# Split values, block means and scale maxima through a buffer in HBM

## The chip, the core and the metric

The kernel runs on one core of a Trainium2 chip. The time is the device time of one execution in microseconds (us). The core has five engines with an instruction queue each: TensorE (PE, with weight loads PEld), VectorE (DVE), ScalarE (ACT), GpSimd (POOL) and SyncE (SP). In this kernel SP computes nothing; it issues every DMA, in one order fixed at build time. An instruction that waits for a semaphore holds up all that stand behind it on its engine. Sixteen DMA engines move the data.

## The reference

Four batches of local attention with block means, then a feed-forward layer with weights shared by all tokens. B=4, H=8, S=768, D=64; 3072 tokens of 512 values; `w_in` 512x2048, `w_out` 2048x512; all float32.

```python
block, window = 32, 16
k_sum = k.reshape(B, H, nb, block, D).max(axis=3)      # 24 blocks of 32 keys
v_sum = v.reshape(B, H, nb, block, D).mean(axis=3)
scores_l = scale * q @ k.T                              # kept where |i-j| < 16
scores_s = scale * q @ k_sum.T + log(block)
a = softmax(concat(scores_l masked, scores_s))
attn = a @ concat(v, v_sum)
h = x @ w_in
out = (h * sigmoid(h)) @ w_out                          # x = attn, heads side by side
```

## The kernel before

A query tile has 128 tokens; it is worked as two halves of 64 (z=0, 1). A half sees 96 neighbouring keys (64 and 15 on either side, and two that pad) and 24 block means: 120 columns. Tiles are numbered s=0 to 23, six per batch (t=0 to 5). Batch 0 is computed in float32; batches 1 to 3 have q, k, values, probabilities and means split into a high and a low float16 part, and three matmuls take the place of one. The split needs a scale, a power of two above the largest magnitude of the batch.

The feed-forward layer takes 12 chunks of 256 tokens. Chunk 0 is float32; from chunk 1 on, weights and activations are split in the same way (line 838 is the first product, 851 the second). Chunks 10 and 11 use a form with seven products in place of eight (lines 926, 968). ACT and DVE compute the activation in between: tanh (863), a product (864), the high part (866), the low part (867).

A planner (`Plan`) sets the order on every engine: each step has a cost for every engine that may run it, the keys that it reads and writes, and a priority from the numbers of `TUNE`; a list scheduler then places the steps, and the order that it finds is the program's order. Its cost for a DMA step is a number in the code, `{"dma": 2100}` for the loads of values below.

Places that the change touches:

- `job_v` (444) makes the block sums of values of a batch from four loads `vR`, their largest magnitude (`am_max`), the scale (`v_scale`), and the split means, which a DMA transpose brings to `vmp` (460).
- `job_vn` (539) loads 256 rows of values (`vP`), splits them and leaves them in SBUF, in `vn_t` (printed as tile `v` in the trace), a ring of two that shares its memory with `v0_t`. A row of split values is 2048 bytes.
- `job_vs` (549) fills `vv` (part of the tile `first`), the value operand of tile s, in two buffers. It issues eight DMAs: four copies SBUF to SBUF out of `vn_t` (15, 81, 79 and 17 rows, the first or last from a zero-padded input at the ends of a batch) and four of 24 rows of means.
- `all_max` (246) takes a maximum over the 128 partitions on POOL. It is called once for the weights, three times for q and k, four times for the values (402, 429, 793).
- `job_a` (line 691) transposes the split probabilities by DMA, four times per tile; `job_c` (724) multiplies them with `vv`.

All inputs of batches 1 to 3 pass through `raw`, a ring of three stages.

Of the kernel before, what the change touches and what calls it, by code (L numbers as in the profile page):

```python
# [10 lines left out]
F32 = mybir.dt.float32  # L11
F32R = mybir.dt.float32r
F16 = mybir.dt.float16
# [46 lines left out]
ALLMAX = 1100  # L60
# [7 lines left out]
class Plan:  # L68
# [58 lines left out]
    def sweep(self, prio, on, back):  # L127
# [18 lines left out]
        while ready:  # L146
# [13 lines left out]
            if e == "pe" and not back:  # L160
                early = early and cols < self.BUSY
# [12 lines left out]
            else:  # L174
                stop = t + cost * (1.0 if e in ("pe", "dma") else self.MARGIN)
# [58 lines left out]
def local_attn_ffn(ctx: ExitStack, tc: tile.TileContext, qkT, qP, qF, kF, v, vR, vP, w, out):  # L234
# [11 lines left out]
    def all_max(out, in_):  # L246
        nc.gpsimd.partition_all_reduce(out, in_, P, bass_isa.ReduceOp.max)

# [3 lines left out]
    const = ctx.enter_context(tc.tile_pool(name="const", bufs=1))  # L252
    psum = ctx.enter_context(tc.tile_pool(name="psum", bufs=1, space=bass.MemoryType.PSUM))
# [52 lines left out]
    vn_t = [t.bitcast(F16).rearrange("p (a i c) -> p a i c", a=2, i=2) for t in v0_t]  # L306
    vmf_t = const.tile([P, 4, P], F16, name="vmf")
# [30 lines left out]
    count = {}  # L338

# [52 lines left out]
    def job_scale(b, prio):  # L392
# [9 lines left out]
        plan.op({"pool": ALLMAX}, lambda e: all_max(qc[:, 0:2], qm_t[:, 7:9]), r=["qm_q", "qm_k"], w=["qc"], prio=prio)  # L402
# [20 lines left out]

    def am_max(n, prio):
        plan.op({"dve": 73}, lambda e: nc.vector.tensor_reduce(out=am_t[:, 7:8], in_=am_t[:, :n], axis=AX.X, op=ALU.max), r=[("am", j) for j in range(n)], w=["am4"], prio=prio)

    def v_scale(b, prio):
        vs = vsc_t[b % 2]
        plan.op({"pool": ALLMAX}, lambda e: all_max(sc2[:, 0:1], am_t[:, 7:8]), r=["am4"], w=["sc2"], prio=prio)
# [14 lines left out]
    def job_v(b, prio):  # L444
# [15 lines left out]
        plan.op({"dma": 1250}, lambda e: nc.sync.dma_start_transpose(out=vmp_t, in_=vmf_t.rearrange("p a b -> p (a b)")), r=["vmf"], w=["vmp"], prio=prio)  # L460
# [78 lines left out]
    def job_vn(b, n, prio):  # L539
# [7 lines left out]
        plan.op({"dve": 1196}, lambda e: nc.vector.scalar_tensor_tensor(out=vn[:, :, 1], in0=flat, scalar=vsc[:, 0:1], in1=vn[:, :, 0], op0=ALU.mult, op1=ALU.subtract), r=key + [("vsc", b % 2)], w=vn_key(g % 2), prio=prio)  # L547

    def job_vs(s, prio):
        prio += nudge("vs", s)  # L550
        b, t = divmod(s, NTILE)
        if b == 0:
            return
        if t == 0:
            job_vn(b, 0, prio)
            job_vn(b, 1, prio)
        if t == 3:
            job_vn(b, 2, prio)
        vv = vv_t[s % 2]
        key = ("vv", s % 2)  # L560

        def rows(z, at, tile, first, n):
            if not 0 <= tile < NTILE:
                return vv[at:at + n, z].rearrange("p i c -> p (i c)").bitcast(F32), v[0, t if z == 0 else NTILE - 1, at:at + n, z, :]
            g = (b - 1) * (NTILE // 2) + tile // 2
            return vv[at:at + n, z], vn_t[g % 2][first:first + n, tile % 2]

        part = P - HALF + HALO
# [7 lines left out]
        slots = {((b - 1) * (NTILE // 2) + x // 2) % 2 for x in (t - 1, t, t + 1) if 0 <= x < NTILE}  # L576
        plan.op({"dma": 2100}, load, r=["vmp", "first"] + [k for x in slots for k in vn_key(x)], w=[key], prio=prio)
# [45 lines left out]
    def job_a(m, prio):  # L623
# [55 lines left out]
        for j, n in enumerate(ns):  # L679
# [11 lines left out]
            plan.op({"dma": 1250}, lambda e, tt=tt, pt=pt: nc.sync.dma_start_transpose(out=tt, in_=pt.rearrange("p a b -> p (a b)")), r=pkeys + ["third"], w=[ttk], prio=prio)  # L691
# [99 lines left out]
    def w_scale(prio):  # L791
        plan.op({"dve": 80}, lambda e: nc.vector.tensor_reduce(out=wx_t, in_=wm_t, axis=AX.X, op=ALU.max), r=[("wm", f, kind) for f in range(NFT) for kind in range(2)], w=["wx"], prio=prio)
        plan.op({"pool": ALLMAX}, lambda e: all_max(wc[:, 0:2], wx_t), r=["wx"], w=["wc"], prio=prio)
# [19 lines left out]
    def job_f(n, c, fs):  # L813
# [12 lines left out]
        def fill():  # L826
            nc.tensor.matmul(out=h[:, :CH], lhsT=unit[:, :P], rhs=unit, start=True, stop=True)

# [26 lines left out]
        for at, f in enumerate(fs):  # L855
            need = [("wf", f, 0)] if c == 0 else [("wh", f, 0), ("wl", f, 0)]
            if n < HALVES:
                for half in range(2):
                    cs = slice(half * P, half * P + P)
                    plan.op({"pe": 900}, ffn1(at, f, cs), r=[("xh", z, half), ("xl", z, half)] + need, w=[("bank", k, half)], prio=i, cols=2048, fill=fill)  # L860
            else:
                plan.op({"pe": 1800 if c == 0 else 1312}, ffn1(at, f, slice(0, CH)), r=xs + need + turn, w=bk(k) if at == 0 else [("bank", k, 1)], prio=i + at, cols=4096 if c == 0 else 3072, fill=fill)
# [66 lines left out]
    def job_fast(n, c, fs):  # L929
# [7 lines left out]
        def fill():  # L937
            nc.tensor.matmul(out=h[:, :CH], lhsT=unit[:, :P], rhs=unit, start=True, stop=True)

        for at, y in enumerate(fs):  # L940
            plan.op({"pe": 1312}, ffn1_pairs(h, at, y, z), r=[(x, z, half) for x in ("xh", "xl") for half in range(2)] + [("wh", y, 0), ("wl", y, 0), ("turn", n - 3)], w=bk(k) if at == 0 else [("bank", k, 1)], prio=i + at, cols=3072, fill=fill)
# [71 lines left out]
    def job_tail(n, c, fs):  # L1013
# [9 lines left out]
        def fill():  # L1023
            nc.tensor.matmul(out=h[:, :CH], lhsT=unit[:, :P], rhs=unit, start=True, stop=True)

        for at, f in enumerate(fs):
            plan.op({"pe": 1312}, ffn1_pairs(h, at, f, z), r=[(x, z, half) for x in ("xh", "xl") for half in range(2)] + [("wh", f, 0), ("wl", f, 0), ("turn", n - 3)], w=bk(k) if at == 0 else [("bank", k, 1)], prio=i + at, cols=3072, fill=fill)
# [132 lines left out]
TUNE = dict(quad=308.75, vd=-86.5, ws=818.0, s0=-738.75, wp=1594.25, wm=33.0, km=-55.75, w_dma=-1.5, w_dec=878.75, a0=-71.0, a1=-119.25, d1=-66.5, span=51.75, post=1866.5, ffn2=5.0, jc0=92.5, jc1=-1748.25, jx0=2.25, jx1=143.0, vs=617.5, qk=305.75, k=-1369.75, v=-54.75, v0=83.75, out=-4.5, first=1452.5)  # L1160
# [61 lines left out]
```

## Time and profile before

| | |
|---|---|
| time, median of 3 runs | 672.36 us (671.85 to 673.94) |
| profiled execution | 674.95 us, span 673.2 us |
| PE busy | 598.7 us, 89% of the span |
| DVE busy | 458.7 us, 68% |
| ACT busy | 342.6 us, 51% |
| POOL busy | 92.9 us, 14% |
| mean granted TensorE clock | 0.953 |

The span is what the trace covers; 1.75 us of the execution lie around it. [...] In the rows below, a time ahead of a row is in us from the span's start, and names such as `L574` are lines of the kernel before.

### The profile page before, as it was taken

How to read it: one execution, taken by the hardware profiler on the slowest of the kernel's cores; microseconds unless marked ns; L12 is line 12 of the kernel's file. 1: busy time of each engine (PE TensorE's matmuls, PEld its weight loads, DVE VectorE, ACT ScalarE, POOL GpSimd, SP SyncE). 2: the span in 40 equal slices, each digit the busy share in tenths (PEclk: the TensorE clock that was granted, in tenths of full speed). 3: DMA queues.
4: the chain of work that ended last, by engine and by line, in shares of the span. 5: the costliest groups of instructions: out<-in, count | busy, mean ns of one | idle time of the engine just before them, and what ended most of it. 6: DMA issues, size and time to landing. Idle time of an engine off the chain costs nothing.

```text
span 673.2 us, 15159 instructions
## 1 busy us (share of the span) xinstructions
PE 598.7 (89%) x5944; PEld 413.3 (61%) x5944; DVE 458.7 (68%) x1243; ACT 342.6 (51%) x837; POOL 92.9 (14%) x183
## 2 busy tenths in 40 slices
PE   8899999799749858996998876999996798999997
PEld 5667666466526525663665543666663566688886
DVE  6799897898074636982773643879857696255655
ACT  4899885565054541651554532545643554234342
POOL 4112002201000000000000000005222420031130
PEclk9999999799969969998999797999997899999999
DMA  8997612237544539636433536474473379000000
GB/s 342 417 418 284 201 56 87 77 101 92 117 129 124 118 123 140 157 81 83 127 98 101 144 72 97 109 183 44 141 78 103 46 88 80 1 32 1 33 1 31
DMA packets 64938, 80.07 MB, mean 119 GB/s; under 512 B 44068, under 2 KB 46052, under 8 KB 63076
## 3 DMA queue, kind: packets, MB, share of 16 engines
q1 hardware_dynamic: 64868, 79.12, 48.0%
q8 instruction: 46, 0.75, 0.5%
q14 instruction: 24, 0.20, 0.1%
HBM read 54.33 MB, written 6.29 MB: 90 GB/s over the span
## 4 chain that ended last, share of the span: by engine, by line
PE 46%; DMA 21%; DVE 15%; ACT 9%; SPq 4%; issue 4%; POOL 0%; DVEq 0%; ACTq 0%
PE bank L851 16%; PE bank L838 15%; DMA first<-v 9%; PE bank L926 6%; DMA raw<-in_qF_dram 6%; PE bank L968 5%; SPq L574 3%; DMA third<-first 2%; DVE wr L789 2%; ACT e L644 2%; DVE wr L773 2%; PE bank L724 1%; PE bank L605 1%; ACT wr L866 1%; DVE first L688 1%
## 5 line engine op out<-in xcount | busy, mean ns | idle before, releaser
L851 PE MATMUL bank<-wr 128*128 128x512 f16 x768 | 193.1, 400 | 52.6 <-ACT wr L866 45.2
L838 PE MATMUL bank<-x,wr 128*128 128x256 f16 x1728 | 205.2, 275 | 1.3 <-DVE work L864 1.3
L838 PEld LDWEIGHTS <-wr 128*128 128x128 f16 x1728 | 169.3, 99 | 38.8 <-issue 3.7
L851 PEld LDWEIGHTS <-wr 128*128 128x128 f16 x768 | 75.0, 101 | 140.3 <-ACT wr L866 47.2
L864 DVE SCALAR_TENSOR_TENSOR wr<-wr,bank 128x512 f32<-128x512 f32 x64 | 43.7, 683 | 67.0 <-ACT wr L863 66.7
L644 ACT ACTIVATE e<-e,mx 128x120 f32<-128x120 f32 x192 | 73.2, 384 | 17.4 <-DVE mx L641 17.3
L863 ACT ACTIVATE wr<-bank,th 128x512 f32<-128x512 f32 x64 | 43.5, 679 | 69.2 <-PE bank L838 69.2
L866 ACT ACTIVATE wr<-wr 128x512 f16<-128x512 f32 x64 | 40.1, 627 | 49.4 <-DVE wr L864 49.3
L867 DVE SCALAR_TENSOR_TENSOR wr<-wr 128x512 f16<-128x512 f32 x64 | 45.9, 717 | 16.1 <-ACT wr L866 15.7
L688 DVE SCALAR_TENSOR_TENSOR first<-e,sum,first 128x120 f16<-128x120 f32 x144 | 44.9, 363 | 4.3 <-POOL first L657 4.1
L657 POOL TENSOR_SCALAR first<-e,sum 128x120 f16<-128x120 f32 x33 | 14.9, 455 | 238.2 <-DVE sum L650 56.4
L926 PE MATMUL bank<-x,wr 128*128 128x256 f16 x384 | 45.8, 273 | 0.1
L641 DVE CUSTOM_DVE_ANT_0 e<-bank,masks,qsc 128x120 f32<-128x120 f32 x144 | 40.2, 338 | 4.5 <-PE bank L605 4.5
L926 PEld LDWEIGHTS <-wr 128*128 128x128 f16 x384 | 37.5, 98 | 5.5 <-issue 0.3
L968 PE MATMUL bank<-wr 128*128 128x256 f16 x315 | 37.7, 273 | 0.0
L644 ACT ACTIVATION_READ_ACCUMULATOR e<-e,mx 128x1 f32 x192 | 36.5, 190 | 0.0
L968 PEld LDWEIGHTS <-wr 128*128 128x128 f16 x315 | 30.7, 98 | 3.6
L848 PE MATMUL bank<-wr,work 128*128 128x512 f32 x64 | 29.2, 594 | 1.6 <-DVE work L864 1.6
L835 PE MATMUL bank<-x,wr 128*128 128x256 f32 (+1 forms) x144 | 29.8, 359 | 0.4 <-issue 0.4
L953 POOL TENSOR_TENSOR wr<-wr 128x128 f32<-128x128 f32 x33 | 18.8, 573 | 76.0 <-DVE wr L953 71.0
L250 POOL TENSOR_TENSOR wr<-wr 128x256 f32<-128x256 f32 x32 | 25.8, 823 | 20.4 <-DVE wr L911 11.6
L851 PE MATMUL bank<-wr,work 128*128 128x512 f16 x96 | 24.2, 395 | 4.7 <-ACT work L866 2.7
(153 smaller groups left out, 760.8 us busy)
## 6 DMA issues: line engine op xcount, KB each, us to landing
wr<-in_w_dram SPq DMA_DIRECT2D x14, 1024.0 KB
raw<-in_qkT_dram SPq DMA_DIRECT2D x18, 576.0 KB
out_dram<-raw SPq DMA_DIRECT2D x23, 256.0 KB
raw<-in_kF_dram SPq DMA_DIRECT2D x12, 384.0 KB
raw<-in_qF_dram SPq DMA_DIRECT2D x9, 512.0 KB
raw<-in_vR_dram SPq DMA_DIRECT2D x12, 384.0 KB
raw<-in_vP_dram SPq DMA_DIRECT2D x9, 512.0 KB
first<-v SPq DMA_DIRECT2D x18, 162.0 KB
```

The source lines that it names most:

```text
L641: plan.op({"dve": 262 if b else 206}, lambda e, i=i, j=j, et=et, mx=mx: nc.vector.tensor_tensor_reduce(out=et[:, i, :], in0=sc[j][:, i, :N ...
L644: plan.op({"act": 385}, lambda e, i=i, j=j, et=et, mx=mx: nc.scalar.activation(out=et[:, i, :], in_=et[:, i, :], func=AF.Exp, scale=-1.0, ...
L688: nc.vector.scalar_tensor_tensor(out=pt[:, i, P:P + NKEY], in0=et[:, i, :], scalar=su4[:, 2 * j + i:2 * j + i + 1], in1=pt[:, i, :NKEY], o ...
L835: nc.tensor.matmul(out=o, lhsT=wi[:, ct * P:(ct + 1) * P], rhs=x0[:, ct, cs], start=(ct == 0), stop=(ct == NCT - 1))
L838: nc.tensor.matmul(out=o, lhsT=wip[:, part, ct * P:(ct + 1) * P], rhs=x[:, ct, :], start=(ct == 0 and q == 0), stop=(ct == NCT - 1 and q = ...
L851: nc.tensor.matmul(out=bank[ob[u]][:, cs], lhsT=g[:, rows], rhs=wop[:, part, cs], start=(begins and q == 0), stop=(stops and q == 2))
L863: plan.op({"act": 51 + 213 * m if c == 0 else 147 + 213 * m}, lambda e: nc.scalar.activation(out=t, in_=h, func=AF.Tanh, scale=0.5 if c == ...
L864: plan.op({"dve": 70 + 267 * m}, lambda e: nc.vector.scalar_tensor_tensor(out=t, in0=t, scalar=1.0, in1=h, op0=ALU.add, op1=ALU.mult), r=b ...
L866: plan.op({"act": 98 + 213 * m}, lambda e: nc.scalar.activation(out=gh, in_=t, func=AF.Copy, scale=SHRINK), r=tk + free, w=ghk, prio=post)
L867: plan.op({"dve": 76 + 267 * m}, lambda e: nc.vector.scalar_tensor_tensor(out=gl, in0=t, scalar=SHRINK, in1=gh, op0=ALU.mult, op1=ALU.subt ...
L926: nc.tensor.matmul(out=h[:, at * CH:at * CH + CH], lhsT=wip[:, p, ct * P:(ct + 1) * P], rhs=x[:, ct, :], start=(ct == 0 and q == 0), stop= ...
L968: nc.tensor.matmul(out=acc_of(c, m)[0], lhsT=x[:, left[m]], rhs=right[m](p), start=(opens and q == 0 and m in (1, 4, 2, 7)), stop=(closes ...
```

## The change

The split values are written to HBM once per 256 rows (`vd`), the split means once per batch (`md`). Tile s then loads its values with one DMA per half, out of `vd`; the mean rows are loaded for the first two tiles of a batch only, one for each buffer of `vv`. The maximum over partitions is a store of one or two numbers per partition to HBM (`sd`), a load of all of them into every partition, and a reduction on DVE. The numbers in `TUNE` are others, so that the planner's order differs everywhere; the early filler matmuls of PE end by another test, and the filler follows the width of what it fills. The rest of the computation is as before.

```diff
-    def all_max(out, in_):
-        nc.gpsimd.partition_all_reduce(out, in_, P, bass_isa.ReduceOp.max)
+    def all_max(out, in_, r, w, prio):
+        i, n = nxt("sd", 2 * B), in_.shape[1]
+        flat, row = sd_t[i].rearrange("p n -> (p n)")[:n * P], vms_t[:, :n * P]
+        plan.op({"dma": 600}, lambda e: nc.sync.dma_start(out=flat.rearrange("(p n) -> p n", n=n), in_=in_), r=r, w=[("sd", i)], prio=prio)
+        plan.op({"dma": 450}, lambda e: nc.sync.dma_start(out=row, in_=flat.unsqueeze(0).to_broadcast([P, n * P])), r=[("sd", i)], w=[("vms", 0)], prio=prio)
+        plan.op({"dve": 65 + 133 * n}, lambda e: nc.vector.tensor_reduce(out=out, in_=row.rearrange("q (p n) -> q n p", n=n), axis=AX.X, op=ALU.max), r=[("vms", 0)], w=w, prio=prio, port=())
...
+        def keep(e):
+            for i in range(2):
+                nc.sync.dma_start(out=md_t[b - 1][:, i], in_=vmp_t[i * BLK:i * BLK + NB].rearrange("p a b -> p (a b)"))
+        plan.op({"dma": 900}, keep, r=["vmp"], w=[("md", b)], prio=prio)
...
+        plan.op({"dma": 1300}, lambda e: nc.sync.dma_start(out=vd_t[b - 1][n * 2 * P:(n + 1) * 2 * P].rearrange("(a p) i c -> p a i c", a=2), in_=vn), r=vn_key(g % 2), w=[("vd", b, n)], prio=prio)
...
-        moves = [rows(0, NB, t - 1, P - HALO, HALO), rows(0, NB + HALO, t, 0, part + 2), rows(1, 0, t, HALF - HALO, part), rows(1, part, t + 1, 0, HALO + 2)]
-        moves += [(vv[rowsm[z], z, i], vmp_t[i * BLK:i * BLK + NB].rearrange("p a b -> p (a b)")) for z in range(2) for i in range(2)]
+        if t < 2:
+            def lead(e):
+                for z in range(2):
+                    nc.sync.dma_start(out=vv[rowsm[z], z], in_=md_t[b - 1])
+            plan.op({"dma": 900}, lead, r=[("md", b), "first"], w=[key], prio=prio)
+        spans = []
+        for z in range(2):
+            a = t * P + z * HALF - HALO
+            lo, hi = max(a, 0), min(a + NKEY - NB, S)
+            spans.append((local[z].start + lo - a, lo, hi))
         def load(e):
-            for o, i in moves:
-                nc.sync.dma_start(out=o, in_=i)
-        plan.op({"dma": 2100}, load, r=["vmp", "first"] + [k for x in slots for k in vn_key(x)], w=[key], prio=prio)
+            for z, (at, lo, hi) in enumerate(spans):
+                nc.sync.dma_start(out=vv[at:at + hi - lo, z], in_=vd_t[b - 1][lo:hi])
+        plan.op({"dma": 1050}, load, r=[("vd", b, n) for n in units] + ["first"], w=[key], prio=prio)
...
-TUNE = dict(quad=308.75, vd=-86.5, ws=818.0, ...
+TUNE = dict(quad=6.75, vd=-1134.25, ws=-4.75, ...
```

Where the order matters to the text below, it reads as follows. On SP at the start of batch 1, before, from the transpose of the means to the second tile's loads (`first` holds `vv` and the split probabilities, `third` the transposed ones, `v_125` and `v_126` the split values):

```order
L460 DMA_TRANSPOSE vmp<-vmf 128x4x128
L478 DMA raw_118<-in_qkT_dram 128x1152
L691 DMA_TRANSPOSE third<-first 128x4x128 x2
L574 DMA first<-in_v_dram 15x512
L574 DMA first<-v_125 81x1024
L574 DMA first<-v_125 79x1024
L574 DMA first<-v_125 17x1024
L574 DMA first<-vmp 24x512 x4
L691 DMA_TRANSPOSE third<-first 128x4x128 x2
L574 DMA first<-v_125 15x1024
```

The same place after the change, from the store of the values' maxima on (`vd_129` is the HBM buffer of batch 1's values, `md_132` that of its means, `sd_138` that of its maxima):

```order
L430 DMA sd_138<-am 128x1
L560 DMA raw_120<-in_vP_dram 128x1024
L431 DMA vms<-sd_138 128x128
L560 DMA raw_118<-in_vP_dram 128x1024
L470 DMA_TRANSPOSE vmp<-vmf 128x4x128
L564 DMA vd_129<-v_127 128x2x1024
L474 DMA md_132<-vmp 24x512 x2
L709 DMA_TRANSPOSE third<-first 128x4x128
L494 DMA raw_120<-in_qkT_dram 128x1152
L709 DMA_TRANSPOSE third<-first 128x4x128
L581 DMA first<-md_132 24x1024 x2
L709 DMA_TRANSPOSE third<-first 128x4x128 x2
```

Right behind these stand the loads of 81 and of 96 rows out of `vd_129`. Eight issues for a tile have become two to four, the maxima's store and load are new on SP, and between the store of the split values and their first load stand two stores of means, four transposes, a load of q and k, and two loads of means.

On DVE at the scale of the weights (`wm` holds the maxima of the weights' tiles, `wc` and `ws` their scale), before:

```order
L792 TENSOR_REDUCE wx<-wm 128x2
L795 TENSOR_SCALAR wc<-wc 128x2
L796 TENSOR_SCALAR wc<-wc 128x2
L797 TENSOR_SCALAR ws<-wc 128x2
L798 RECIPROCAL ws<-ws 128x2
```

And after the change, where line 432 is the new reduction:

```order
L810 TENSOR_REDUCE wx<-wm 128x2
L879 SCALAR_TENSOR_TENSOR work<-work,bank_186 128x512
L381 TENSOR_REDUCE km_151<-raw_119 128x24
L432 TENSOR_REDUCE wc<-vms 128x2
L813 TENSOR_SCALAR wc<-wc 128x2
```

Two other steps now stand between the two; the one of them is a product of the activation (line 864 before), the other the reduction of a load of k (line 378 before).

## Rows read from the trace of the kernel before

**Rows 1.** The page: busy time, then granted clock in 40 slices.
```profile
PE 598.7 (89%) x5944; PEld 413.3 (61%) x5944; DVE 458.7 (68%) x1243; ACT 342.6 (51%) x837; POOL 92.9 (14%) x183
...
PEclk9999999799969969998999797999997899999999
```

**Rows 2.** Busy time in two stretches of the span, all engines.
```profile
core 0: us, PE busy (x) PEld busy (x) DVE busy (x) ACT busy (x) POOL busy (x), PEclk, DMA share, GB/s
0.00:126.00 126.00, 114.13 (x1034) 78.09 (x1035) 110.50 (x262) 97.81 (x216) 24.79 (x67) 0.99 0.64 241
126.00:570.00 444.00, 385.35 (x4027) 252.63 (x4026) 296.46 (x886) 209.75 (x564) 49.30 (x83) 0.93 0.54 108
```

**Rows 3.** The same view, eight stretches at half clock: the first and the sum.
```profile
183.90:197.50 13.60, 3.60 (x9) 1.14 (x9) 8.93 (x34) 7.03 (x23) 0.67 (x1) 0.50 0.45 143
...
sum 53.90, PE 31.55 PEld 12.74 DVE 35.63 ACT 26.62 POOL 6.53; mean PE 3.94 PEld 1.59 DVE 4.45 ACT 3.33 POOL 0.82
```

**Rows 4.** Waits of PE: who was waited for, us, times, longest.
```profile
PE bank L851 <- ACT wr L866: 45.2, 8, 13.1
PE bank L851 <- DVE wr L867: 7.3, 5, 4.4
```

**Rows 5.** The chain that ended last: start us, us, what.
```profile
75.04 3.65 DMA raw<-in_qF_dram
...
154.36 10.39 DMA first<-v
166.33 10.44 DMA first<-v
...
183.71 4.83 DMA first<-v
...
209.25 9.15 DMA raw<-in_qF_dram
...
384.58 12.02 DMA first<-v
398.40 2.19 DMA first<-vmp
```

**Rows 6.** SP's own time line around the first two loads of batch 1.
```profile
152.64 2.47 SPq L574 DMA_DIRECT2D first<-v  x3
155.15 3.06 SPq L574 DMA_DIRECT2D first<-vmp  x4
...
163.38 3.63 SPq L574 DMA_DIRECT2D first<-v  x4
```

**Rows 7.** PE's time line around its longest wait.
```profile
178.00 2.78 PE L838 MATMUL bank<-x,wr 128*128 128x256 f16 x24
193.90 3.89 PE L851 MATMUL bank<-wr 128*128 128x512 f16 x9 [13.12 <-ACT wr L866]
```

**Rows 8.** DVE's time line at the scale of the weights.
```profile
76.94 0.18 DVE L792 TENSOR_REDUCE wx<-wm 128x2 f32<-128x32 f32 x1
77.74 0.17 DVE L795 TENSOR_SCALAR wc<-wc 128x2 f32<-128x2 f32 x1 [0.62 <-POOL wc L247]
```

**Rows 9.** Groups of instructions: count, busy us, mean ns.
```profile
L864 DVE SCALAR_TENSOR_TENSOR work<-work,bank 128x512 f32<-128x512 f32 x15 | 10.2, 681 | 1.1 <-ACT work L863 1.0
L378 DVE TENSOR_REDUCE km<-raw 128x24 f32<-128x768 f32 x12 | 11.2, 948 | 21.2 <-DMA raw<-in_kF_dram 21.2
L399 DVE TENSOR_REDUCE qm<-qm 128x1 f32<-128x3 f32 x3 | 0.5, 151 | 0.0
```

**Rows 10.** Busy time in two stretches in which PE never waits.
```profile
280.00:300.00 20.00, 20.00 (x219) 13.22 (x218) 18.16 (x57) 11.04 (x30) 1.10 (x3) 1.00 0.46 122
420.00:440.00 20.00, 20.00 (x185) 13.77 (x183) 17.93 (x55) 10.59 (x31) 0.36 (x1) 1.00 0.43 118
```

**Rows 11.** The pool's and the DVE's work at the scale of batch 1.
```profile
116.06 0.37 POOL L247 PARTITION_ALL_REDUCE qc<-qm  x1 [5.90 <-issue]
116.31 3.85 POOL L1078 MEMSET first<- 128x512 f16 x8
```

More of the change, by code (lines that the diff above doesn't have):

```diff
@@ L6 @@
 import concourse.tile as tile
-from concourse import bass_isa, mybir
+from concourse import mybir
 from concourse.masks import make_identity
@@ L59 @@
 EARLY = 40
-ALLMAX = 1100
 PACE = 4
@@ L160, in sweep @@
             if e == "pe" and not back:
-                early = early and cols < self.BUSY
+                early = early and not self.ops[i][6]
                 if early or self.ops[i][6]:
@@ L306, in local_attn_ffn @@
     vn_t = [t.bitcast(F16).rearrange("p (a i c) -> p a i c", a=2, i=2) for t in v0_t]
+    vd_t = [far.tile([S, 2, DM], F16, name=f"vd{i}") for i in range(B - 1)]
+    md_t = [far.tile([NB, 2, DM], F16, name=f"md{i}") for i in range(B - 1)]
+    sd_t = [far.tile([P, 2], F32, name=f"sd{i}") for i in range(2 * B)]
     vmf_t = const.tile([P, 4, P], F16, name="vmf")
@@ L338, in local_attn_ffn, with idle @@
     count = {}
+    def idle(o):
+        return lambda: nc.tensor.matmul(out=o, lhsT=unit[:, :P], rhs=unit[:, :o.shape[1]], start=True, stop=True)
     def nxt(tag, n):
@@ L553, in job_vs @@
             return
[L554 to L568, printed above, removed]
-        moves = [rows(0, NB, t - 1, P - HALO, HALO), rows(0, NB + HALO, t, 0, part + 2), rows(1, 0, t, HALF - HALO, part), rows(1, part, t + 1, 0, HALO + 2)]
-        moves += [(vv[rowsm[z], z, i], vmp_t[i * BLK:i * BLK + NB].rearrange("p a b -> p (a b)")) for z in range(2) for i in range(2)]
+        j = s % 2
+        vv, key = vv_t[j], ("vv", j)
+        if s == NTILE:
+            plan.op({"pool": 1000, "dve": 550}, lambda e: eng[e].memset(vv[:HALF, 0], 0.0), r=["first"], w=[key], prio=prio)
+        for n in ((0, 1), (), (2,), (), (), ())[t]:
+            job_vn(b, n, prio)
+        if t < 2:
[8 more added lines that the diff above has]
+            spans.append((local[z].start + lo - a, lo, hi))
         def load(e):
-            for o, i in moves:
-                nc.sync.dma_start(out=o, in_=i)
-        slots = {((b - 1) * (NTILE // 2) + x // 2) % 2 for x in (t - 1, t, t + 1) if 0 <= x < NTILE}
-        plan.op({"dma": 2100}, load, r=["vmp", "first"] + [k for x in slots for k in vn_key(x)], w=[key], prio=prio)
+            for z, (at, lo, hi) in enumerate(spans):
+                nc.sync.dma_start(out=vv[at:at + hi - lo, z], in_=vd_t[b - 1][lo:hi])
+        units = {x // (2 * P) for _, lo, hi in spans for x in (lo, hi - 1)}
+        plan.op({"dma": 1050}, load, r=[("vd", b, n) for n in units] + ["first"], w=[key], prio=prio)
     def heads(g):
@@ L690, in job_a @@
             plan.op({"dve": 510}, low, r=[sum_key(j, i) for i in range(2)] + [("e", n, i) for i in range(2)], w=pkeys, prio=prio)
-            plan.op({"dma": 1250}, lambda e, tt=tt, pt=pt: nc.sync.dma_start_transpose(out=tt, in_=pt.rearrange("p a b -> p (a b)")), r=pkeys + ["third"], w=[ttk], prio=prio)
+            plan.op({"dma": 1290}, lambda e, tt=tt, pt=pt: nc.sync.dma_start_transpose(out=tt, in_=pt.rearrange("p a b -> p (a b)")), r=pkeys + ["third"], w=[ttk], prio=prio)
     def job_c(m, prio):
@@ L935, in job_fast @@
         h = bank[k]
-        def fill():
-            nc.tensor.matmul(out=h[:, :CH], lhsT=unit[:, :P], rhs=unit, start=True, stop=True)
         for at, y in enumerate(fs):
-            plan.op({"pe": 1312}, ffn1_pairs(h, at, y, z), r=[(x, z, half) for x in ("xh", "xl") for half in range(2)] + [("wh", y, 0), ("wl", y, 0), ("turn", n - 3)], w=bk(k) if at == 0 else [("bank", k, 1)], prio=i + at, cols=3072, fill=fill)
+            plan.op({"pe": 1312}, ffn1_pairs(h, at, y, z), r=[(x, z, half) for x in ("xh", "xl") for half in range(2)] + [("wh", y, 0), ("wl", y, 0), ("turn", n - 3)], w=bk(k) if at == 0 else [("bank", k, 1)], prio=i + at, cols=3072, fill=idle(h[:, at * CH:at * CH + CH]))
         t = area(4 * j + 3, 0, F32)
@@ L1021, in job_tail @@
         release("tail", tk + ghk + glk, post)
-        def fill():
-            nc.tensor.matmul(out=h[:, :CH], lhsT=unit[:, :P], rhs=unit, start=True, stop=True)
         for at, f in enumerate(fs):
-            plan.op({"pe": 1312}, ffn1_pairs(h, at, f, z), r=[(x, z, half) for x in ("xh", "xl") for half in range(2)] + [("wh", f, 0), ("wl", f, 0), ("turn", n - 3)], w=bk(k) if at == 0 else [("bank", k, 1)], prio=i + at, cols=3072, fill=fill)
+            plan.op({"pe": 1312}, ffn1_pairs(h, at, f, z), r=[(x, z, half) for x in ("xh", "xl") for half in range(2)] + [("wh", f, 0), ("wl", f, 0), ("turn", n - 3)], w=bk(k) if at == 0 else [("bank", k, 1)], prio=i + at, cols=3072, fill=idle(h[:, at * CH:at * CH + CH]))
         for at in range(2):
```

17 lines of the change are left out of this document (8 added, 9 removed).

## The prediction

> **What bounds the kernel now.** I read the page's busy times and slices first. PE is busy for 598.7 us, 89%, and no other engine is above 68%; the granted clock falls below full in slice after slice of the middle [rows 1]. So PE is the bound where it runs, and the question is what makes it stop. The view by stretches splits that: in the first 126 us PE misses 126 - 114.13 = 11.9 us at clock 0.99; in the 444 us behind them it misses 444 - 385.35 = 58.65 us at clock 0.93 [rows 2]. Most of the idle time is therefore in batches 1 to 3. Eight stretches there, 53.9 us together, ran at half clock, and PE was busy for 31.55 us of them [rows 3]; the first began while PE waited, and it had been busy until then [rows 3, 7]. At full clock that work takes half, so the stretches cost 15.8 us more. Idle time and slow clock together: 58.65 + 15.8 = 74.4 us.
>
> The waits of PE name ACT line 866 eight times, 45.2 us, and DVE line 867 five times, 7.3 us [rows 4]. These only hand on a wait: the longest, 13.12 us from 180.8 on [rows 7], comes in the chain right behind loads of values. There, two copies of `first<-v` take 10.39 and 10.44 us from issue to landing, one later on 12.02 us [rows 5]. SP's time line tells which they are. It issues three copies from 152.64 on, which by the order are those of 81, 79 and 17 rows; the one issued last, at 154.36, is the one of 17 rows, 34 KB [rows 5, 6]. The same line at 183.71 is a copy of 81 rows, more than four times as large, and took 4.83 us [rows 5]. So size does not make the delay; the copy of 17 rows stands behind that of 79. Nothing of the next tile's loads is issued before 163.38 [rows 6]. Other traffic is caught too: a load of q of 512 KB lands after 3.65 us at 75.04, in the first 126 us where none of these copies runs, and after 9.15 us at 209.25 in the midst of them [rows 5]. Every one of the 18 tiles of batches 1 to 3 has this pair. What ends the middle's waits, I conclude, is one slow copy per tile: it holds `vv`, every DMA behind it, SP, and through late q, k and values DVE, ACT and PE.
>
> **The change part by part.**
>
> *Loads of values.* The change gives a half 96 rows in one DMA. At a batch's first tile the lower half has 81 rows, as 15 lie outside; at its last tile the upper half has 79 (from row 5 x 128 + 64 - 15 = 689 to 768). The copies of 17 and 15 rows are gone, and of the 18 loads of 79 rows three stay, one per batch. No copy of 96 rows is in the trace. Its nearest rows are 4.83 us for 81 rows and 3.65 us for a load of 128 rows; the ends are 2.19 us, the smallest copy seen, and 12.02 us, the slowest [rows 5]. I take about 4 us, by the first two, since 96 rows lie between them. The 74.4 us over 18 tiles make 4.13 us each. Fifteen tiles lose it, 62.0 us; three keep it, 12.4 us.
>
> [...]
>
> *SP's own time.* Seven issues take 2.47 + 3.06 = 5.5 us of a tile [rows 6], some 0.8 us each; two take some 1.6 us. SP is not on PE's path where its DMAs land, so I count nothing beyond the stalls above.
>
> *The way through HBM.* New are nine stores of split values (512 KB), three pairs of stores of means and twelve loads of means. A load of values now waits for a store's landing. No store of this size has a row; a load of as many bytes took 3.65 us, and 9.15 us when caught [rows 5]. The order puts nine DMAs between the first store and its first load, two stores of means, four transposes, a load of q and k and two loads of means, so the wait is covered there, and I take nothing. Without that cover nine waits of 3.65 us and three of 2.19 us for the means cost 39.4 us of SP, with the transposes of the probabilities queued behind.
>
> *The maxima.* Eight times a store, a load and a DVE reduction replace POOL's instruction. For each DMA I take 2.19 us, the row of the smallest copy; the ends are the same row's time with the second hidden, and 9.15 us [rows 5]. A reduction of 128 numbers lies between 151 ns for 3 and 948 ns for 768 [rows 9], in proportion 0.28 us, and 0.41 us for two times 128: 4 x 0.28 + 4 x 0.41 = 2.8 us of DVE in all, which has room (68%). Where it matters is the weights' scale, which every product of chunk 1 waits for: there the wait before was 0.62 us [rows 8]. Now it is 2 x 2.19 + 0.41 = 4.8 us; the two steps placed in it cover 0.68 + 0.95 = 1.6 us [rows 9]; it grows by 4.8 - 1.6 - 0.6 = 2.6 us. The ends are -0.6 and 2 x 9.15 + 0.4 - 1.6 - 0.6 = 16.5 us; I take 2.6 us, by the row at which the queue is not caught. At the scale of batch 1 POOL needed 5.90 us before it began its instruction, and its memsets then ran for 3.85 us [rows 11]; two landings need 4.4 us. A small gain is likely there, and I count it as nothing.
>
> *Planner, priorities and fillers.* The numbers of matmuls are the same, so PE's work is. In stretches without a slow copy PE runs all of 20 us with DVE at 18.16 and 17.93 us [rows 10], so a changed order has little to win there. I count nothing.
>
> **The sum.** 674.95 - 62.0 + 2.6 = 615.6 us for the profiled execution, which stood 2.6 us above the median of 672.36. Against the median: 613 us.
>
> **The rivals.**
>
> *DVE takes over (644 us).* DVE has 296.46 us of work in the 444 us [rows 2]; with 62 us taken out it is busy for 78% on the average, and where PE runs freely for 90% [rows 10]. If its queue is late at every second tile, half of the gain returns as waits for lines 864 to 867: 613 + 31 = 644 us. For it: [rows 10]. Against it: in those very stretches PE does not wait.
>
> *All slow copies go (596 us).* The loads of 79 rows land when there is nothing behind them that PE needs, and the batch scales cost less than now: 613 - 12.4 - 4.5 = 596 us. For it: these are now single, with full queues on either side. Against it: four transposes of the same tile stand right behind each.
>
> *The way through HBM is exposed (690 us, slower).* One mechanism: SP, in order, waits for the landing of what it has just stored, and the transposes of probabilities stand behind. Eight maxima at 2 x 2.19 us are 35.0 us, and the stores of values and means 39.4 us as above. All exposed: 613 + 74.4 = 687, with the DVE reductions 690 us. It decides above 59.4 us of these, four fifths. For it: at every maximum the order has few DMAs between store and load. Against it: most other places are filled.
>
> *It doesn't do what it says (673 us).* Loads of 96 rows out of HBM are as slow as the pair of copies, say 10.4 us each, and the waits stay. For it: no such load is in the trace. Against it: the load of 128 rows at 75.04.
>
> **How the numbers follow.** The sum as worked out 0.62, with its own range of 600 to 628 us; DVE takes over 0.20; all slow copies go 0.11; exposed 0.05; no effect 0.02. The range of 598 to 645 us holds all of the first but a little, six in ten of the second, half of the third: 0.61 + 0.12 + 0.05, about 8 in 10. A measurement of this kernel tells 0.3% from no change; faster is 0.62 + 0.20 + 0.11 = 0.93, the same 0.02, slower 0.05.
>
> **What would show it right or wrong.** Right: no load of values above 6 us on the chain but three at most, at the last tiles of the batches; loads of q below 5 us there; PE misses under 20 us between 126 us and the end of attention, and at most three stretches at half clock. The step on maxima: SP waiting for a landing ahead of each load of `vms`, and some 5 us from the last weight's maximum to the scale. Wrong: PE waits as long as now but for DVE whose queue never empties (DVE takes over), or SP waits for its own stores with transposes behind (exposed), or loads of 96 rows of about 10 us.

## The result, and the profile after

The changed kernel takes 624.26 us (median of four, 621.29 to 625.27) beside 672.48 us for the kernel before (671.85 to 673.94): a ratio of 0.927, interval 0.924 to 0.931. The forecast was 613 us with a range of 598 to 645 us. Sign and range held; the gain is 48 us where the sum had 59, so one term or more has the wrong size. The profiled execution took 621.29 us, its span 619.6 us. Of the experiments below one execution, of 821.29 us in the run with slow widths, is left out of median and ratio, as it was over 1.5% longer than the fastest of its kernel.

The page of the changed kernel, busy time and then granted clock in 40 slices:

```profile
PE 586.8 (95%) x5944; PEld 411.1 (66%) x5944; DVE 448.1 (72%) x1220; ACT 343.2 (55%) x844; POOL 103.1 (17%) x200
...
PEclk9899998999899999899999999998999999999999
```

The count of matmuls is that of [rows 1]. PE's idle time falls from 673.2 - 598.7 = 74.5 us to 619.6 - 586.8 = 32.8 us, by 41.7 us, and its busy time by 11.9 us, since fewer matmuls run at the lower clock: the mean granted clock is 0.983 instead of 0.953. The two make the 53.6 us by which the span is shorter.

Busy time in the two stretches of [rows 2], the changed kernel (us, then busy us and instruction count of each engine, granted clock, DMA share, GB/s):

```profile
core 0: us, PE busy (x) PEld busy (x) DVE busy (x) ACT busy (x) POOL busy (x), PEclk, DMA share, GB/s
0.00:126.00 126.00, 111.57 (x1000) 76.44 (x1001) 102.06 (x254) 92.16 (x200) 24.69 (x65) 0.96 0.68 243
126.00:570.00 444.00, 429.56 (x4538) 294.79 (x4536) 317.06 (x913) 234.89 (x617) 68.95 (x117) 0.99 0.55 119
```

Behind 126 us PE now misses 14.4 us where it missed 58.65 us. In the first 126 us it misses 14.4 us, 2.6 us more than before, and the clock there went from 0.99 to 0.96: this stretch, which holds the scale of the weights, got worse.

Three short stretches at half clock remain behind 126 us, where there were eight with 53.9 us [rows 3]:

```profile
155.70:159.10 3.40, 3.01 (x8) 1.09 (x9) 3.40 (x19) 2.54 (x11) 0.00 (x0) 0.51 0.40 154
258.10:261.50 3.40, 2.92 (x7) 0.99 (x8) 2.94 (x12) 1.82 (x4) 0.00 (x0) 0.51 0.96 320
425.40:428.80 3.40, 3.40 (x9) 1.22 (x8) 3.40 (x17) 3.21 (x11) 0.00 (x0) 0.50 0.00 0
```

Where PE waits, by who is waited for (total us, times, longest), answers to [rows 4]:

```profile
PE bank L863 <- DVE work L879: 6.9, 2, 6.3
PE bank L866 <- ACT wr L881: 5.3, 2, 2.7
PE bank L866 <- DVE sc L442: 4.3, 1, 4.3
PE bank L866 <- DVE sc L441: 2.4, 1, 2.4
```

ACT's line 866 of before is line 881 now: 45.2 us have become 5.3 us. The first row stood at 1.6 us before (line 848 waiting for line 864); the third and fourth are new. Line 879 is a product of the activation of chunk 0, which stands on DVE behind the scale of the weights; `sc` on lines 441 and 442 is the scale of a batch's values. All three hang on a maximum that now goes through HBM.

The chain that ended last answers to [rows 5] (start us, us, what):

```profile
386.58 9.44 DMA raw<-in_vR_dram
...
411.10 7.84 DMA sd<-am
418.96 5.26 DMA vms<-sd
```

No load of split values is among its longest pieces. What it has instead is one load that takes 9.44 us, and a maximum of values: its store of 512 bytes lands after 7.84 us, and the load of it after another 5.26 us, 13.1 us where I had taken 2 x 2.19.

SP's time line around that first piece, the changed kernel (start us, us, issue):

```profile
383.80 0.33 SPq L459 DMA_DIRECT2D raw<-in_vR_dram  x1
384.23 0.72 SPq L592 DMA_DIRECT2D first<-vd  x2
386.58 0.36 SPq L459 DMA_DIRECT2D raw<-in_vR_dram  x1
389.92 0.35 SPq L494 DMA_DIRECT2D raw<-in_qkT_dram  x1
390.42 6.91 SPq L709 DMA_TRANSPOSE third<-first  x4
```

The two issues at 384.23 are the loads of the batch's last tile, of 96 and of 79 rows; the load of 9.44 us stands right behind them. So a load of 79 rows out of HBM still holds what follows it, as the forecast had it for these three. PE stands still behind two of them, for 2.70 us and 2.65 us.

The scale of the weights, DVE of the changed kernel (answers to [rows 8]):

```profile
80.58 0.19 DVE L810 TENSOR_REDUCE wx<-wm 128x2 f32<-128x32 f32 x1
80.68 0.68 DVE L879 SCALAR_TENSOR_TENSOR work<-work,bank 128x512 f32<-128x512 f32 x1
81.49 0.95 DVE L381 TENSOR_REDUCE km<-raw 128x24 f32<-128x768 f32 x1
90.09 0.42 DVE L432 TENSOR_REDUCE wc<-vms 128x2 f32<-128x256 f32 x1 [7.64 <-DMA vms<-sd]
```

and SP in the same place:

```profile
80.80 0.33 SPq L430 DMA_DIRECT2D sd<-wx  x1
84.77 0.33 SPq L431 DMA_DIRECT2D vms<-sd  x1
```

From the end of the last maximum to the end of the new reduction it is 90.51 - 80.77 = 9.7 us where the sum had 4.8: the store took some 4.0 us, the load some 5.3 us. The reduction itself is as estimated, 0.42 us for 0.41. DVE waits 7.64 us at the reduction, and a float32 product of chunk 0 stands behind it. PE's row that ends this:

```profile
94.88 3.37 PE L863 MATMUL bank<-wr,work 128*128 128x512 f32 x4 [6.31 <-DVE work L879]
```

The values' maximum of batch 1, SP of the changed kernel:

```profile
140.61 0.33 SPq L430 DMA_DIRECT2D sd<-am  x1
142.95 0.33 SPq L560 DMA_DIRECT2D raw<-in_vP_dram  x1
150.06 0.33 SPq L431 DMA_DIRECT2D vms<-sd  x1
```

Here the store holds SP until 150.06, 9.45 us after its issue, and not only for its own load: SP issues nothing else between 143.3 and 150.06 us. Over the whole kernel SP waits so ahead of seven of the eight loads of maxima (us in total, times, longest):

```profile
SPq L431 <- DMA sd<-am: 25.9, 3, 14.7
SPq L431 <- DMA sd<-qm: 12.2, 3, 4.4
SPq L431 <- DMA sd<-wx: 3.6, 1, 3.6
```

### The profile page after: what moved, and what is told of

It is laid out like the page before. It is cut to its first block, busy times and chain, and to the rows that moved or that the text cites. A ratio compares the mean times of both kernels' runs of the same rounds, so it can differ in the third digit from the quotient of the medians.

```text
span 619.6 us, 15088 instructions
## 1 busy us (share of the span) xinstructions
PE 586.8 (95%) x5944; PEld 411.1 (66%) x5944; DVE 448.1 (72%) x1220; ACT 343.2 (55%) x844; POOL 103.1 (17%) x200
## 5 line engine op out<-in xcount | busy, mean ns | idle before, releaser
L853 PE MATMUL bank<-x,wr 128*128 128x256 f16 x1728 | 201.8, 273 | 0.5 <-DVE x L760 0.5
L866 PE MATMUL bank<-wr 128*128 128x512 f16 x768 | 183.3, 384 | 8.4 <-ACT wr L881 5.3
L675 POOL TENSOR_SCALAR first<-e,sum 128x120 f16<-128x120 f32 x47 | 21.0, 455 | 171.4 <-ACT e L662 37.3
L941 PE MATMUL bank<-x,wr 128*128 128x256 f16 x384 | 44.4, 273 | 0.0
L863 PE MATMUL bank<-wr,work 128*128 128x512 f32 x64 | 31.1, 621 | 6.9 <-DVE work L879 6.9
L241 POOL TENSOR_SCALAR second<-ks 128x384 f16<-128x384 f16 x14 | 7.5, 538 | 163.4 <-PE bank L623 110.1
L965 POOL TENSOR_TENSOR wr<-wr 128x128 f32<-128x128 f32 x41 | 23.0, 571 | 55.7 <-DVE wr L965 39.0
L850 PE MATMUL bank<-x,wr 128*128 128x256 f32 (+1 forms) x144 | 31.7, 376 | 0.1
L850 PEld LDWEIGHTS bank<-x,wr 128*128 128x128 f32 x144 | 26.1, 206 | 5.5 <-issue 2.2
```

Source lines behind the costliest of these rows:

```text
L850: nc.tensor.matmul(out=o, lhsT=wi[:, ct * P:(ct + 1) * P], rhs=x0[:, ct, cs], start=(ct == 0), stop=(ct == NCT - 1))
L853: nc.tensor.matmul(out=o, lhsT=wip[:, part, ct * P:(ct + 1) * P], rhs=x[:, ct, :], start=(ct == 0 and q == 0), stop=(ct == NCT - 1 and q = ...
L866: nc.tensor.matmul(out=bank[ob[u]][:, cs], lhsT=g[:, rows], rhs=wop[:, part, cs], start=(begins and q == 0), stop=(stops and q == 2))
L941: nc.tensor.matmul(out=h[:, at * CH:at * CH + CH], lhsT=wip[:, p, ct * P:(ct + 1) * P], rhs=x[:, ct, :], start=(ct == 0 and q == 0), stop= ...
```

## The experiments

Each run stands beside the kernel before on the same chip (672.5 to 672.8 us in all three groups), so the ratios compare. The changed kernel's ratio is 0.927.

**Only the widths, in the kernel before.** Each copy of 79 rows is made in 64 and 15, each of 17 in 16 and 1; out of SBUF as before, in the old order.

```diff
-                nc.sync.dma_start(out=o, in_=i)
+                cut = {79: 64, 17: 16}.get(o.shape[0], o.shape[0])
+                nc.sync.dma_start(out=o[:cut], in_=i[:cut])
+                if cut < o.shape[0]:
+                    nc.sync.dma_start(out=o[cut:], in_=i[cut:])
```

> The kernel before, with its copies of values inside SBUF cut so that no copy has 79 or 17 rows: 64 and 15 in place of 79, 16 and 1 in place of 17. Ten copies per tile instead of eight, the planner and its order as before. Theory (the number of rows decides how many DMA engines share a copy, and one slow copy per tile makes the waits): the pair lands within 4 us of its issue instead of over 10, PE's idle time from 126 to 570 us falls from 58.65 us below 25 us, and the time falls by 40 to 60 us, to 612 to 632. Rival (copies inside SBUF are slow, the way through HBM is what helps): within 1% of 672. Rival (the number of DMA issues on SP is what counts): two more issues of about 0.8 us per tile make it slower, 672 to 690. Rival (the new order by the new numbers makes the gain): within 1% of 672.

Measured: 638.93 us, 0.949 (0.945 to 0.953), 34 us less although it issues 36 DMAs more. Busy time from 126 to 570 us:

```profile
126.00:570.00 444.00, 414.75 (x4305) 277.69 (x4306) 311.28 (x915) 223.09 (x592) 55.45 (x93) 0.97 0.43 109
```

PE misses 29.25 us instead of 58.65 us, and its clock is 0.97 instead of 0.93. Of the copies of values one stands among the longest pieces of the chain, and it lands after 1.93 us. Number of rows alone, with no HBM and no other order, makes the larger part of the gain. It does not make all that I had put on it: 34 us, not 74.4, and less than the 40 to 60 us expected of this run; PE's idle time stayed above the 25 us expected.

**Slow widths in the changed kernel.** Every load of values is split at row 79, so 96 rows become 79 and 17.

```diff
-                nc.sync.dma_start(out=vv[at:at + hi - lo, z], in_=vd_t[b - 1][lo:hi])
+                for x, y in ((lo, lo + 79), (lo + 79, hi)):
+                    if y > x:
+                        nc.sync.dma_start(out=vv[at + x - lo:at + y - lo, z], in_=vd_t[b - 1][x:y])
```

> The changed kernel with every load of 96 rows out of HBM cut into 79 and 17 rows, and 81 into 79 and 2; all else, the order too, as changed. Theory (width of the load): the waits return, 18 tiles with 79 rows in each half instead of one, so at least as many as before: 665 us or more. Rival (it is the way through HBM or the fewer DMAs that helps): two more issues per tile of about 0.4 us each, 620 to 632. Rival (the new order): the same, 620 to 632.

Measured: 792.85 us (median of three), 1.176 (1.169 to 1.183), 18% slower than the kernel before. Its chain and its busy time:

```profile
172.31 14.68 DMA first<-vd
...
216.31 12.21 DMA raw<-in_qkT_dram
```

```profile
126.00:570.00 444.00, 311.27 (x3011) 200.88 (x3010) 212.93 (x639) 161.64 (x437) 26.66 (x59) 0.84 0.54 93
```

PE misses 132.7 us at clock 0.84. Out of HBM such loads are at least as slow as copies within SBUF were (14.68 us beside 10.4 to 12.0 us on the chain of before), and other loads (`qkT`, 12.21 us) are caught by them. There are two pairs for a tile here, one for each half, where before had one. So the source of a copy isn't what made it slow.

**The three loads of 79 rows.** In the changed kernel they alone are split, in 64 and 15.

```diff
+                cut = lo + 64 if hi - lo == 79 else hi
+                for x, y in ((lo, cut), (cut, hi)):
...
```

> The changed kernel with its last three slow loads cut, 64 and 15 rows in place of 79. Theory as I priced it in the sum: 4.13 us each, 12.4 us, so 612 us. By the waits of the profile after (idle times of PE of 2.69 and 2.64 us right behind two of them, each with a stretch at half clock, none behind the third): 2.7 + 2.6 + 1.5 + 0 = about 7 us, so 617. Rival (they are hidden, the waits there have another cause): within 0.3% of 624.

Measured: 611.59 us, 0.908 (0.906 to 0.911): 12.7 us less than the changed kernel, where the sum had 12.4 us for these three.

```profile
126.00:570.00 444.00, 436.27 (x4624) 302.75 (x4623) 322.86 (x924) 237.94 (x623) 70.31 (x121) 1.00 0.50 119
```

PE misses 7.7 us behind 126 us, half of what it missed. In all three runs the time goes with the number of rows: -34 us with the copies of 79 and 17 rows split, +169 us with such loads in every tile, -13 us with the last three split.

The trace shows how such copies land: it records steps of a semaphore for each DMA. In the changed kernel each of the 30 loads of 96 rows makes 16 steps, all some time after its issue; each of 81 rows makes one as it is issued and nine later; each of the three of 79 rows makes one as it is issued and one single step 9.0 to 10.3 us after it. In the kernel before, all copies of 79 and 17 rows out of SBUF make one and one, too, the late one 9.6 to 12.4 us after the issue, and so do all loads of 79 and 17 rows in the run with slow widths. The copies with a single late step are the slow ones.

The share of the 16 DMA engines that is busy tells the two kinds apart as well. In the kernel before, from 162.5 to 163.2 us, while the first copies of 79 and 17 rows near their landing (163.3 and 164.8 us) and little else moves, the share is 0.06, about one engine of the 16, at 23 GB/s. In the changed kernel, from 478.9 to 479.4 us, while two loads of 96 rows are under way, it is 0.96 at 320 GB/s.

**The maxima back on POOL.** The changed kernel with the same order, but each maximum made by POOL's instruction in the place of the reduction; its store and its load issue nothing.

```diff
-        ... lambda e: nc.sync.dma_start(out=flat..., in_=in_) ...
-        ... lambda e: nc.sync.dma_start(out=row, in_=flat...) ...
-        ... lambda e: nc.vector.tensor_reduce(out=out, in_=row...) ...
+        ... lambda e: None ...
+        ... lambda e: None ...
+        ... lambda e: nc.gpsimd.partition_all_reduce(out, in_, P, bass_isa.ReduceOp.max) ...
```

> The changed kernel with the eight maxima made by the pool engine again, in place of the store, the load and the reduction; the planner still counts these three, so that the order of everything else is that of the changed kernel. Theory (the maxima's way through HBM is the term that I sized too small: 4 to 17 us per store where I took 2.19): PE's idle times of 6.31, 4.31 and 2.43 us at 88.6, 151.8 and 422.8 us go or shrink, with the half clock behind them 8 to 16 us less, 608 to 616. Rival (these waits come from DVE's and ACT's queue, not from the maxima): within 0.5% of 624.

Measured: 608.44 us, 0.904 (0.901 to 0.907), 15.8 us less than the changed kernel. The way of the maxima through HBM costs 15.8 us more than POOL's instruction where the sum had 2.6 us: this is the term of the wrong size.

```profile
0.00:126.00 126.00, 118.08 (x1054) 81.20 (x1054) 108.11 (x271) 96.71 (x212) 26.34 (x68) 0.99 0.65 246
126.00:570.00 444.00, 433.17 (x4596) 301.14 (x4597) 318.79 (x903) 234.87 (x611) 71.22 (x130) 0.99 0.51 116
```

The spans of the two profiled executions differ by 619.6 - 607.2 = 12.4 us: 6.5 us are idle time of PE in the first 126 us (7.9 us instead of 14.4 us), where the clock is 0.99 again, 3.6 us are idle time in the stretch behind, and 2.2 us PE's busy time (584.6 us on the page), by the clock.

**How small a store may be.** Two runs store the values' maximum of a batch with more columns than the one that is needed, so that each partition writes 8 or 16 bytes instead of 4; the reduction reads one column. The stores for weights, q and k (8 bytes) stay. The edit below is of the run with 16 bytes; the other has `m = 2`.

```diff
+        m = 4 if n == 1 else n
+        src = am_t[:, 8 - m:8] if n == 1 else in_
```

> The changed kernel with the maxima of the values (four of the eight) stored as two numbers per partition, 8 bytes instead of 4; the second is the maximum, the first a zero that no one reads. In the profile after the four stores of 4 bytes landed after 7.8 to 17.4 us, the four of 8 bytes after 4.0 to 5.0 us. Theory (bytes per partition set how long the store takes): the four stores of values land after some 4 to 5 us outside the weights' loading, the idle times of PE at 151.8 and 422.8 us (4.31 and 2.43 us) shrink, 3 to 9 us less: 615 to 621. Rival (the traffic around them makes them late): landings as they are, within 0.3% of 624.

> The same with 16 bytes per partition (three zeros and the maximum). Theory (bytes per partition): landings of 2.5 to 4 us and the time at or below that of the version with 8 bytes. If only 4 bytes are special, as the one with 8 bytes. Rival (traffic around): as the changed kernel.

Measured: 609.24 us, 0.906 (0.903 to 0.909), with 8 bytes; 607.73 us, 0.905 (0.902 to 0.908), with 16. SP at the same maximum, first with 8 bytes:

```profile
137.05 0.33 SPq L432 DMA_DIRECT2D sd<-am  x1
139.39 0.33 SPq L562 DMA_DIRECT2D raw<-in_vP_dram  x1
139.96 0.33 SPq L433 DMA_DIRECT2D vms<-sd  x1
```

then with 16:

```profile
137.53 0.33 SPq L432 DMA_DIRECT2D sd<-am  x1
139.87 0.33 SPq L562 DMA_DIRECT2D raw<-in_vP_dram  x1
140.29 0.38 SPq L433 DMA_DIRECT2D vms<-sd  x1
```

From store to load it is 9.45 us with 4 bytes for each partition, 2.91 us with 8, 2.76 us with 16. By the steps of their semaphores the stores landed after 9.4, 2.9 and 1.4 us; with 16 bytes the load of the maxima is held by the issue of a load of values before it, and no longer by the store. The store delays that load of values (512 KB) too: it landed 9.9, 4.8 and 3.6 us after its issue. The stores of more bytes landed sooner, and four stores made wider win 15.0 and 16.5 us, more than the 3 to 9 us expected and as much as taking all eight off the way. These two runs keep one cost that POOL's run hasn't, the wait at the weights, so POOL's run should have a cost of its own; PE waits 4.2 us there for a product on POOL (line 674), but what makes that product late was not shown. The wait at the weights, with 16 bytes:

```profile
PE bank L865 <- DVE work L881: 6.1, 1, 6.1
```

So the values' maxima make the larger part of the cost, and the sum had counted these as nothing and looked at the weights alone.

**Is the way of the values free?** Every store of split values is issued twice, the first time to a buffer that nobody reads.

```diff
...
+            for t in (vx_t, vd_t):
+                nc.sync.dma_start(out=t[b - 1][n * 2 * P:(n + 1) * 2 * P].rearrange("(a p) i c -> p a i c", a=2), in_=vn)
```

> The changed kernel with every store of split values to HBM made twice, first to a second buffer that no one reads: nine more DMAs of 512 KB. In my sum the way of the values through HBM costs nothing, as other work covers it: within 0.5% of 624 (some 0.4 us of SP per store, 3.6 us in all, hidden too). Rival (the store and its landing are on PE's path): the landings of 3.0 to 7.1 us grow by 1.3 us or more each (512 KB at some 400 GB/s), 9 x 1.3 = 12 us: 632 to 640.

Measured: 629.29 us, 0.934 (0.931 to 0.938), 5 us more than the changed kernel, with intervals that just touch; PE misses 18.2 us behind 126 us instead of 14.4 us. Neither answer fits well (the 400 GB/s of the second is near the highest of the page's slices, 417 GB/s): if the difference is real, nine stores of 512 KB cost about half a microsecond each, not nothing and not a landing.

**The number of DMAs.** Two runs have the widths mended and the maxima on POOL. The first is that alone; the second makes the loads of a tile in some ten pieces, none of 79 or 17 rows and all out of HBM: it cuts the rows at 15 in the one half and at 64, 79 and 95 in the other, and from the third tile of a batch on loads four blocks of means.

```diff
+                ends = [c for c in ((15,), (64, 79, 95))[z] if c < hi - lo]
+                for x, y in zip([0] + ends, ends + [hi - lo]):
+                    nc.sync.dma_start(out=vv[at + x:at + y, z], in_=vd_t[b - 1][lo + x:lo + y])
...
```

> The changed kernel with the three loads of 79 rows cut into 64 and 15 and the maxima on the pool engine. If the two repairs add up by the waits of the profile after: 624 - 7 - 12 = 605 us, 600 to 612. If what remains late behind them takes their place: 612 to 618. Rival (neither is on the path): 622 to 626.

> The version with 64 and 15 rows and the maxima on the pool engine (603.4 us), but with the loads of each tile cut into as many DMAs as the cut version of the kernel before has: 15 and 81, 64, 15, 16 and 1 rows, and four loads of means, none of them on few engines for long. Ten issues per tile instead of two to four, all of them from HBM, the order as changed. The cut version of the kernel before took 638.9 us. Theory (what is left between 639 and 603 is the number of DMAs): 620 to 640. Rival (it is the planner's new order): 601 to 608. In between if the issues are cheaper from HBM (0.4 us each here, against 0.7 to 0.8 us out of SBUF): 608 to 615.

Measured: 603.37 us, 0.897 (0.894 to 0.900), and 622.15 us, 0.924 (0.919 to 0.929). The two repairs together bring 20.9 us, not 12.7 + 15.8 = 28.5 us. A part of that is seen: with the maxima on POOL alone, PE's waits behind two loads of 79 rows are already down to 1.85 and 1.23 us from 2.70 and 2.65 us, so less is left to mend. The rest was not told apart; with padded stores in place of POOL the two repairs nearly add up, as the last run shows. The pieces cost 18.8 us, though that run's four executions lie between 616.9 and 625.7 us; this is in the range of the theory that counts DMAs. The source line of the loads, its issues in the run with pieces (ns, least, median, most):

```profile
L593 SPq DMA_DIRECT2D first<-vd x102: 214/388/1794, 163.0 to 523.6; - x102
```

and in the changed kernel:

```profile
L592 SPq DMA_DIRECT2D first<-vd x36: 241/380/1387, 169.8 to 526.4; - x36
```

An issue costs SP 0.38 us either way. The copies inside SBUF of the kernel before cost twice as much:

```profile
L574 SPq DMA_DIRECT2D first<-v x66: 640/743/1437, 152.6 to 552.0; - x66
L574 SPq DMA_DIRECT2D first<-in_v_dram x6: 536/648/1000, 152.0 to 552.7; - x6
```

But the second row is a load out of HBM, on the same line of that kernel, and a store of split values out of SBUF to HBM is issued in 0.42 us at the median. So it is not the source alone that makes an issue dear.

**The order.** The kernel with both repairs, planned by the numbers in `TUNE` of before.

```diff
-TUNE = dict(quad=6.75, vd=-1134.25, ws=-4.75, ...
+TUNE = dict(quad=308.75, vd=-86.5, ws=818.0, ...
```

> The version with 64 and 15 rows and the maxima on the pool engine, planned with the numbers of the kernel before in TUNE, so that the order differs everywhere. Theory (the order has little to win where nothing is slow): 600 to 610. Rival (the new numbers are a good part of the gain): 615 to 640.

Measured: 612.1 us, 0.910 (0.908 to 0.912), 8.7 us more than with the new numbers and between the two ranges expected. The order is worth something, and the sum had nothing for it. (By these numbers the planner also places 25 more filler matmuls, 79 instead of 54, all early.)

**Both repairs without POOL.** The changed kernel with 64 and 15 rows for 79, and with 16 bytes for each partition in all eight stores of maxima; the columns added for weights, q and k are zeros.

```diff
+                cut = lo + 64 if hi - lo == 79 else hi
...
-        all_max(qc[:, 0:2], qm_t[:, 7:9], ["qm_q", "qm_k"], ["qc"], prio)
+        all_max(qc[:, 0:2], qm_t[:, 7:11], ["qm_q", "qm_k"], ["qc"], prio)
```

> The changed kernel with the three loads of 79 rows cut into 64 and 15, and all eight maxima stored as 16 bytes per partition (padded with zeros that no one reads). Both repairs keep the way through HBM. If they add up: 624.3 - 12.7 - 16.5 = 595 us; the scale of the weights now stores 16 bytes too, and the idle time of PE of 6.1 us behind it should shrink by 2 to 3 us. If the reloading of maxima (3.8 to 5 us) still holds PE there: 597 to 601. Rival (the repairs fill the same gaps): 603 to 608.

Measured: **596.29 us**, 0.886 (0.884 to 0.888): 28 us below the changed kernel, 76 us below the one before, and below both kernels in every run. Here the repairs nearly add up, 28.0 us for 12.7 + 16.5. The same stretch, and then PE's longest wait:

```profile
126.00:570.00 444.00, 443.88 (x4731) 313.26 (x4730) 332.33 (x927) 242.33 (x625) 74.95 (x129) 1.00 0.48 121
```

```profile
PE bank L870 <- DVE work L886: 4.8, 1, 4.8
```

PE misses 0.12 us in 444 us, at full clock, with DVE busy for 75%. That also answers the rival by which DVE takes over: in this stretch nothing but PE bounds the kernel. The wait at the weights is left, shorter by 1.5 us than in the changed kernel.

## Why the prediction was right, and where its sizes failed

**One slow copy per tile: right.** In the trace a copy of 79 or 17 rows lands in one late step, 9.0 to 12.4 us after its issue, where 96 rows make sixteen, the last after 3.6 us at the median. The widths alone give 34 us in the kernel before, slow widths cost 169 us in the changed one, and the three that stayed cost 12.7 us for a forecast of 12.4 us. The two rivals by which the copies' speed hangs on something else fall: the loads of 96 rows came near the 4 us that I had taken, and the three of 79 rows did not become harmless. That the three loads of 79 rows out of HBM stay slow was my estimate, as no run ahead of the forecast shows such a load; the runs after it showed landings after 9.0 to 10.3 us. That 12.7 us came so near is in part luck: the price of 4.13 us for each comes from the division of the next paragraph, which fails.

**62.0 us for it: right in sum, wrong in what it is made of.** Without the maxima's cost the change is worth 672.8 - 608.4 = 64.4 us, close to 62.0, and that is luck. The step that put all idle time and all slow clock of the middle, 74.4 us, on the slow copies fails: mended alone, in the kernel before, they gave 34 us. With all of them mended, the difference from before to the repaired kernel (69.4 us) is 34 us of widths, 19 us of fewer DMAs and 9 us of order, as three runs have them one by one, each in another kernel; 8 us are not separated, and the shorter issue of the new loads is a candidate, not tried by itself. A bound worked out by dividing what is idle by the number of tiles holds everything that is late there, not one cause.

**SP's own time, "nothing": wrong.** Ten issues for a tile instead of two to four cost 19 us, over 18 tiles about 1 us each. The run with pieces shows the price; whether it is SP's issue time, at which loads, transposes and stores stand in one line, or the DMA engines' own work on more and smaller copies was not told apart.

**The order, "nothing": wrong by 9 us.** The stretches at full pace [rows 10] showed that little is to be won in them; they did not show the places between.

**The way of the values through HBM, "nothing": nearly.** Nine DMAs stand between the first store and its first load, no wait of PE names it, and SP's loads of values waited for buffers that PE held (36.3 us, five times) and for no store; a second store costs some 5 us. This bears on the rival of the exposed way: for the values it is out, for the maxima it came true in part, for 15.8 us of its 35.0.

**The maxima, +2.6 us: the step that failed.** I took 2.19 us for each DMA, from a copy of 24 KB in rows of 1 KB [rows 5], as the nearest in size. A store of 4 bytes from each of 128 partitions is much smaller and took 7.84 us on the chain; the load into all partitions took 5.26 us. The second error is the place: I priced the weights' scale alone and let POOL's 5.90 us of waiting [rows 11] pay for the batches. In batch 3 the two landings came to 13.1 us, and PE waited at two of the values' scales, each with a stretch at half clock behind it. At the weights PE's wait grew from 1.3 to 6.3 us, by 5.0 us and not 2.6, and it was not a product of chunk 1 that waited, but one of chunk 0 that stood on DVE behind the reduction. The end that I had written down for the weights alone, 16.5 us, is the size of the whole. What was missing was a row of a store with a few bytes in each partition; without one, both ends belonged in the sum's own range with equal right. The lower end was miscounted besides: with one landing left it is 2.19 + 0.41 - 1.6 - 0.6 = 0.4 us, and -0.6 leaves out both. The middle of 0.4 and 16.5 would have made the forecast 619 us.

**The signs that were named.** No load of values above 6 us on the chain but three at most: so, as none is on it; off the chain the three of 79 rows took 9.0 to 10.3 us, and five of the 30 of 96 rows over 6 us. Loads of q below 5 us: none is on the chain, but of the six behind 126 us three took 5.4 to 6.1 us. SP waiting for a landing ahead of the loads of `vms`: at seven of eight. PE's miss under 20 us behind 126 us: 14.4. At most three stretches at half clock: three, but two of them stand behind a values' maximum (155.7 and 425.4) and only one behind a load of 79 rows. Some 5 us from the last weight's maximum to the scale: 9.7 us, which is the sign that showed the failing step first.

## What to carry to other kernels

Look at the number of rows of a DMA before its bytes: here loads of 79 rows landed after 9.0 to 10.3 us and loads of 96 rows after 3.6 us at the median, and splitting the copies of 79 and 17 rows in two won 34 us in the kernel before, those of 79 rows 12.7 us in the changed one. A value that is stored only to be read back at once may be worth padding: here 8 or 16 bytes for each partition in place of 4 won 15.0 and 16.5 us, and what stands behind its load on the same queue belongs to its price. And when all idle time of a stretch is divided by the number of its tiles, the result is a bound for everything that repeats with the tiles; an edit that removes one of these gets a part of it.

## What the runs showed of the hardware

- A load or copy of 96 rows was reported in 16 steps, one of 81 rows in nine, of 24 rows in twelve, of 79 or 17 rows in a single one, not counting a step at the issue. Loads of 79 rows landed after 9.0 to 10.3 us, of 96 rows after 3.6 us at the median, of 64 rows after 2.9 to 4.1 us.
- A store of 4, 8 and 16 bytes from each of 128 partitions to HBM landed after 9.4, 2.9 and 1.4 us in the same place of the program, and after 7.8, 3.0 and 1.6 us at the last maximum of values.
- Four loads of one row of 512 bytes into all 128 partitions landed after 3.8 to 5.3 us.
- An issue on SP took 0.38 us at the median for a load of split values out of HBM and 0.74 us for a copy of them inside SBUF; stores of them from SBUF to HBM took 0.42 us.
